# A spectral filter with a gated convolution on one core: inverse-transform pairs and double-block gate taps

## The chip, the cores and the metric

One Trainium2 chip, one of its cores. The metric is device microseconds of one execution of the whole program; a kernel's time is the median of its runs.

## What is computed

The input `x` is 8 sequences of 3200 positions with 256 features. Each sequence goes through a real Fourier transform over positions, a complex 256x256 matrix product with a bias in the frequency domain, a soft threshold, and the inverse transform; the result is then gated and projected:

```python
X = np.fft.rfft(x, axis=1)
Yr = Xr @ w_r - Xi @ w_i + b_r
Yi = Xr @ w_i + Xi @ w_r + b_i
Yr = np.sign(Yr) * np.maximum(np.abs(Yr) - 0.01, 0.0)
Yi = np.sign(Yi) * np.maximum(np.abs(Yi) - 0.01, 0.0)
y = np.fft.irfft(Yr + 1j * Yi, n=3200, axis=1)
gate_pre = sum(conv_w[k] * y_shifted_by(4 - k) for k in range(5))   # causal, per feature
out = ((1 / (1 + np.exp(-gate_pre))) * (y @ w_val)) @ w_out
```

All of it is in float32; the wide products run on rounded high and low parts.

## The kernel before, in words

The length 3200 is split as 64 x 50, so each transform has two steps with a transposition through DRAM between them. For each sequence:

- `p1` (8 pieces): the 50-point step. Matmuls on half of the array (L541) into a PSUM tile `p`, an ACT copy (L546) to `s`, a store to `a_dram`.
- `p2` (13 pieces `u`: 12 of two frequencies, a last one of one): load `a`, the 64-point step `s` (L588), the split of its result into high and low parts (`sx`, `xs`, L638 to L650, on ACT and DVE), the frequency product `k_ps` and `y_ps` (L663, L658), bias and sum on DVE (L669, L672), the soft threshold `tp` (an ACT relu, L676, and a DVE operation, L678), the 64-point step back `z_ps` (L694, 64x64 tiles of the array; L687 for the last piece), an ACT copy to `z_t` (L699) and a store to `z_dram`.
- `positions` (8 blocks `k` of 400 positions): load `zl`, the 50-point step back `y_p` (L746), an ACT copy into `y_sb` (L753). The last block is computed first, since the causal window of block 0 begins with its end (the turn: L759, L765).
- `gated` (8 blocks): split of the block into `y_hl`, value product `v_ps` (L778, or L774 with whole float32 weights for the last blocks of the program), five taps per feature half into `acc` (the first on ACT, L804; four on DVE, L807), sigmoid (L817, ACT), gate (L819, DVE), split into `gated` (L313, L315), projection `o_ps` (L778), copy (L843), store.

Nothing runs in the order in which it is written. `Plan` collects all pieces, each with a due place `at`, an assumed duration and its dependences; `Plan.order` then lists them engine by engine: the piece that can begin first, and of those that begin about together the one that is due first. The table `O` holds the offsets of the due places (in units of one `u`), `SLOTS` the number of buffers per kind. Five kinds of PSUM tile, `p`, `z_ps`, `y_p`, `v_ps` and `o_ps`, rotate through the two buffers of `ps_2`. Pieces of mode "q" use tiles of 64 rows of the array (`p`, `z_ps`, `y_p`), all others the whole array. Stages of neighbouring sequences overlap: while sequence b is in `p2`, b+1 is in `p1` and b-1 in `gated`. `WARM` says how many matmuls on zeros keep TensorE busy in five places of the start (L871).

Of the kernel before, what the change touches and what calls it, by code (L numbers as in the profile page):

```python
# [213 lines left out]
CLOCK = ((40000, 1.6), (55000, 1.15))  # L214
# [37 lines left out]
WARM = 2, 1, 1, 1, 6
SLOTS = {"x": 3, "zl": 3, "y_hl": 2, "s1": 2, "a": 3, "xs": 2, "sx": 2, "xz": 1, "yb": 2, "tp": 2, "zst": 3,
# [7 lines left out]
def fourier_filter_then_gated_conv(ctx: ExitStack, tc: tile.TileContext, x, w_r, w_i, b_r, b_i,  # L261
# [300 lines left out]
    def p2(b, u, at):  # L562
# [119 lines left out]
        gs = [("g1", ts[0], 0)]  # L682

        def s1i():
            p = two_banks(kz)
# [3 lines left out]
            g = g1_sb[:, ts[0] * P:(ts[0] + 2) * P].rearrange("p (r q) -> p r q", r=2)

            for r in range(2):
                for i in range(2):
                    for e in range(2):
                        nc.tensor.matmul(p[e * HP:(e + 1) * HP, i, 0:D], g[i * HP:(i + 1) * HP, r, e * HP:(e + 1) * HP],  # L694
                                         tl[kt][i * HP:(i + 1) * HP, r, :], start=r == 0, stop=r == 1)
        add(at + O["s1i"], "PE", 430 if last else 914, s1i, [kt + (0,), *gs], [kz + (0,)], {kz: "ps_2"}, mode="f" if last else "q")
# [83 lines left out]

    def gated(b, k, at):
        bk = (b, k)
        here, there = [("y", k, 0)], [("y", k - 1, j) for j in range(3 if k == 0 else 1)]
        ky, kg, kv, kh, kp, ko = (("y_hl", bk), ("acc", bk), ("v_ps", bk), ("gated", bk), ("o_ps", bk), ("o", bk))
# [3 lines left out]
        else:  # L788
# [10 lines left out]
        acc = lambda c: tl[kg][:, c, :]  # L799

        def first(c):
            if c == 0:
                buffer(kg, "acc", [P, 2, TB])
            nc.scalar.mul(block(acc(c)), y_at(k, c, 0), cw_sb[:, c, 0:1])  # L804

        def tap(c, j):
            nc.vector.scalar_tensor_tensor(out=block(acc(c)), in0=y_at(k, c, j), scalar=cw_sb[:, c, j:j + 1],  # L807
                                           in1=block(acc(c)), op0=ALU.mult, op1=ALU.add)
        for c in range(2):
# [137 lines left out]
```

## Time and profile before

| | |
|---|---|
| median of 3 runs (lowest to highest) | 911.27 us (909.95 to 912.53) |
| the profiled execution, its own time | 911.79 us |
| span of its trace | 909.7 us |
| mean granted TensorE clock | 0.981 of full speed |
| instructions in the trace | 25018 |
| DMA | 162.30 MB, mean 178 GB/s |

The span runs from the first to the last instruction; the execution's own time has 2.1 us more around it. Engines: PE is TensorE, PEld its weight load, DVE VectorE, ACT ScalarE, POOL GpSimd, SP the engine that issues most transfers. Busy time is the union of an engine's instructions; bars of neighbouring instructions overlap by their start-up, so what one costs is read from the distance between starts.

### The profile page before, as it was taken

The numbers are of one execution on the slowest core, as the hardware profiler recorded it, in microseconds if no ns is written. First come the engines' busy times: TensorE is split into PE (matmuls) and PEld (weight loads), VectorE is DVE, ScalarE is ACT, GpSimd is POOL, SyncE is SP. The second block draws the span as 40 slices with busy tenths as digits, with TensorE's granted clock in tenths as the row PEclk, the third lists the DMA queues.
The fourth block names the chain that finished last, engine by engine and source line by source line (L and its number), as shares of the span: only waits on it lengthen the run. The fifth ranks groups of instructions, "written<-read, shape, count | busy, mean of one in ns | idle before, by whom it ended". The sixth has DMA issues, their size and how long they took to land.

```text
span 909.7 us, 25018 instructions
## 1 busy us (share of the span) xinstructions
PE 875.9 (96%) x10362; PEld 739.8 (81%) x10362; DVE 793.9 (87%) x1387; ACT 628.9 (69%) x1096; POOL 4.3 (0%) x11
## 2 busy tenths in 40 slices
PE   7899989999999999999999999999999999999997
PEld 2478767888888979898888888888888998998765
DVE  1256887999998997999799997999889998999796
ACT  1356556878777777877678766877677766876664
POOL 0000000000000000000000000000001000000000
PEclk8799999999999999999999999999999999999999
DMA  6677767544774466735766376644764344423412
GB/s 202 210 247 232 198 208 247 195 157 162 248 242 149 136 217 201 232 129 164 232 209 198 111 226 214 211 159 147 240 203 145 125 154 145 136 74 130 151 60 90
DMA packets 104212, 162.30 MB, mean 178 GB/s; under 512 B 9922, under 2 KB 78404, under 8 KB 104100
## 3 DMA queue, kind: packets, MB, share of 16 engines
q1 hardware_dynamic: 103140, 157.44, 54.3%
q10 hardware_dynamic: 960, 3.28, 1.1%
q8 instruction: 81, 1.33, 0.7%
q14 instruction: 31, 0.25, 0.1%
HBM read 82.04 MB, written 78.64 MB: 177 GB/s over the span
## 4 chain that ended last, share of the span: by engine, by line
PE 45%; DVE 41%; ACT 5%; issue 4%; DMA 3%; ACTq 0%; SPq 0%; DVEq 0%
DVE acc L807 16%; PE y_ps L658 8%; PE o_ps L778 7%; PE v_ps L778 6%; PE s L588 6%; PE z_ps L694 5%; PE k_ps L663 4%; DVE acc L819 4%; PE p L541 3%; PE y_p L746 3%; DVE gated L315 3%; DVE yb L669 3%; DVE yb L672 3%; DVE y_hl L315 2%; DVE xs L646 2%
## 5 line engine op out<-in xcount | busy, mean ns | idle before, releaser
L807 DVE SCALAR_TENSOR_TENSOR acc<-y_sb,cw_sb,acc 128x400 f32<-128x400 f32 x512 | 301.5, 640 | 3.6 <-ACT acc L804 3.4
L778 PE MATMUL o_ps<-gated,wo_sb 128*128 128x400 f32 x756 | 155.2, 355 | 4.0 <-ACT z_t L699 2.5
L658 PE MATMUL y_ps<-w_sb,xs 128*128 128x256 f32 x1152 | 151.7, 281 | 0.2 <-DVE yb L672 0.2
L778 PEld LDWEIGHTS o_ps<-gated,wo_sb 128*128 128x128 f32 x756 | 136.7, 191 | 12.2 <-ACT z_t L699 6.3
L658 PEld LDWEIGHTS y_ps<-w_sb,xs 128*128 128x128 f32 x1152 | 145.3, 190 | 1.6 <-DVE tp L678 0.8
L778 PE MATMUL v_ps<-y_hl,wv_sb 128*128 128x400 f32 x660 | 133.1, 350 | 2.5 <-ACT s L546 0.9
L588 PEld LDWEIGHTS s<-f_sb,a 128*128 128x128 f32 x800 | 102.6, 193 | 35.9 <-issue 24.4
L778 PEld LDWEIGHTS v_ps<-y_hl,wv_sb 128*128 128x128 f32 x660 | 117.1, 188 | 5.8 <-ACT z_t L699 1.6
L588 PE MATMUL s<-f_sb,a 128*128 128x128 f32 x800 | 118.8, 287 | 1.8 <-DMA a<-a_dram 1.8
L694 PE MATMUL z_ps<-tp,g_sb 64*64 64x256 f32 x1536 | 106.2, 393 | 4.3 <-DVE tp L678 4.3
L676 ACT ACTIVATE tp<-yb,nlam 128x512 f32<-128x512 f32 (+1 forms) x104 | 73.5, 706 | 39.9 <-DVE yb L672 38.8
L313 ACT CAST gated<-acc 128x800 fp32r<-128x800 f32 x63 | 54.3, 862 | 55.5 <-DVE acc L819 55.1
L663 PE MATMUL k_ps<-w_sb,xs 128*128 128x256 f32 x576 | 91.2, 294 | 0.0
L678 DVE SCALAR_TENSOR_TENSOR tp<-yb,tp 128x512 f32<-128x512 f32 (+1 forms) x104 | 69.9, 673 | 20.9 <-ACT tp L676 20.8
L817 ACT ACTIVATE acc<-acc 128x400 f32<-128x400 f32 x128 | 67.9, 539 | 25.5 <-DVE acc L807 24.5
L699 ACT COPY z_t<-z_ps 128x512 f32<-128x512 f32 (+1 forms) x104 | 58.7, 565 | 35.7 <-PE z_ps L694 31.6
L663 PEld LDWEIGHTS k_ps<-w_sb,xs 128*128 128x128 f32 x576 | 75.8, 191 | 8.6 <-issue 4.0
L804 ACT ACTIVATE acc<-y_sb,cw_sb 128x400 f32<-128x400 f32 x128 | 75.6, 626 | 10.5 <-DVE gated L315 10.5
L746 PEld LDWEIGHTS y_p<-g_sb,zl 50*64 50x64 f32 x4096 | 68.3, 136 | 17.1 <-ACT z_t L699 6.3
L672 DVE TENSOR_TENSOR yb<-y_ps,yb 128x512 f32<-128x512 f32 x96 | 66.4, 692 | 10.9 <-PE y_ps L658 10.4
L694 PEld LDWEIGHTS z_ps<-tp,g_sb 64*64 64x64 f32 x1536 | 50.3, 134 | 30.4 <-DVE tp L678 3.9
L746 PE MATMUL y_p<-g_sb,zl 50*64 50x50 f32 x4096 | 70.8, 219 | 4.2 <-DVE acc L819 2.2
(79 smaller groups left out, 1027.9 us busy)
## 6 DMA issues: line engine op xcount, KB each, us to landing
zl<-z_dram SPq DMA_DIRECT2D x128, 200.0 KB
out<-o SPq DMA_DIRECT2D x63, 400.0 KB
a<-a_dram SPq DMA_DIRECT2D x96, 256.0 KB
z_dram<-z_t SPq DMA_DIRECT2D x96, 256.0 KB
x<-in_x SPq DMA_DIRECT2D x120, 200.0 KB
a_dram<-s SPq DMA_DIRECT2D x120, 200.0 KB
x<-in_x ACTq DMA_DIRECT2D x8, 200.0 KB
a_dram<-s ACTq DMA_DIRECT2D x8, 200.0 KB
```

Source lines behind the costliest of these rows:

```text
L588: nc.tensor.matmul(spec()[:, c, :, i, :], tl[ka][:, i, c * P:(c + 1) * P], f2_of(i), start=True, stop=True)
L658: nc.tensor.matmul(p[:, 1 - r, :], xm(hx, c, r), w_sb[:, m, hw, c, :], start=k == 0, stop=k == 5)
L663: nc.tensor.matmul(p, sm(hx, c), w_sb[:, 0, hw, c, :], start=k == 0, stop=k == 5)
L672: add(at + 0.2, "DVE", dve(2 * D), lambda: nc.vector.tensor_tensor(out=yb(), in0=tl[ky], in1=yb(), op=ALU.add), [ky + (0,)], [kb + (0,)])
L676: nc.scalar.activation(out=buffer(kt, "tp", [P, 2, D])[:, 0:n], in_=tl[kb][:, 0:n], func=AF.Relu, bias=nlam)
L678: add(at + 0.2, "DVE", dve(n * D), lambda: nc.vector.scalar_tensor_tensor(out=tl[kt][:, 0:n], in0=tl[kb][:, 0:n], scalar=LAM, in1=tl[kt][: ...
L694: nc.tensor.matmul(p[e * HP:(e + 1) * HP, i, 0:D], g[i * HP:(i + 1) * HP, r, e * HP:(e + 1) * HP], tl[kt][i * HP:(i + 1) * HP, r, :], star ...
L746: nc.tensor.matmul(pv[h][e * HP:(e + 1) * HP, c, m, :], zt[half(h), m, c * P + e * HP:c * P + (e + 1) * HP], g2_sb[half(h), :], start=True ...
L778: nc.tensor.matmul(p[:, e, 0:TB], w[:, hw, c, e * P:(e + 1) * P], src(hy, c), start=n == 0, stop=n == 5)
L804: nc.scalar.mul(block(acc(c)), y_at(k, c, 0), cw_sb[:, c, 0:1])
L807: nc.vector.scalar_tensor_tensor(out=block(acc(c)), in0=y_at(k, c, j), scalar=cw_sb[:, c, j:j + 1], in1=block(acc(c)), op0=ALU.mult, op1=A ...
L817: add(at + O["conv"] + 0.15, "ACT", act(TB, "sigmoid"), lambda c=c: nc.scalar.activation(out=acc(c), in_=acc(c), func=AF.Sigmoid), (), [kg ...
```

## The change

Three things change, and the order with them.

1. The step back is made for two pieces at once. For even `u` nothing is issued; for odd `u` one PSUM tile takes 16 matmuls (of `u - 1` and `u`), one ACT copy moves 1024 elements instead of two that move 512, and one store carries 512 KB instead of two of 256 KB. The 13th piece stays alone.
2. The gate's taps and sigmoid run over two neighbouring blocks: `acc` holds 2 x 2 x 400 elements per partition, each tap and each sigmoid has 800 elements instead of 400. The gate's product, the split and the projection stay per block. The last two blocks of the last sequence stay single.
3. The offsets in `O`, the number of warm-up matmuls in the last of the five places (6 to 10), two buffer counts (`tp` 2 to 3, `zst` 3 to 2, the latter now twice as large) and the planner's assumptions on the clock are other numbers, and `gated` is entered two blocks at a time.

```diff
-CLOCK = ((40000, 1.6), (55000, 1.15))
+CLOCK = ((40000, 1.6), (45000, 1.15))
...
-O = {'hold': 0.0, 'together': 2.0, 'later': 4.0,
+O = {'hold': -1.089,
+     'together': 2.272,
+     'later': 4.406,
...
-     's1i': 1.087,
+     's1i': 1.333,
...
-     'conv': 1.033,
-     'val': 1.634,
-     'gate': -3.715,
-     'project': 3.74,
+     'conv': 1.176,
+     'val': 2.74,
+     'gate': -3.751,
+     'project': 5.91,
...
-WARM = 2, 1, 1, 1, 6
...
+WARM = 2, 1, 1, 1, 10
...
+        if u % 2 == 0 and not last:
+            return
+
+        both = (u,) if last else (u - 1, u)
+        kts = [("tp", (b, v)) for v in both]
...
+            for j, v in enumerate(both):
+                g = g1_sb[:, 2 * v * P:(2 * v + 2) * P].rearrange("p (r q) -> p r q", r=2)
+
+                for r in range(2):
+                    for i in range(2):
+                        for e in range(2):
+                            nc.tensor.matmul(p[e * HP:(e + 1) * HP, i, j * D:(j + 1) * D],
+                                             g[i * HP:(i + 1) * HP, r, e * HP:(e + 1) * HP],
+                                             tl[kts[j]][i * HP:(i + 1) * HP, r, :], start=r == 0, stop=r == 1)
...
-            nc.scalar.copy(out=buffer(ko, "zst", [P, 2, D])[:, 0:n], in_=tl[kz][:, 0:n, 0:D])
+            zt = buffer(ko, "zst", [P, 4, D])
...
+            nc.scalar.copy(out=zt.rearrange("p (j i) d -> p i j d", i=2), in_=tl[kz].rearrange("p i (j d) -> p i j d", j=2))
...
-            dst = tl[kd].rearrange("q (m c) -> (q m) c", c=D).rearrange("(t r) c -> r t c", r=P)
-            nc.sync.dma_start(out=dst[:, ts[0]:ts[-1] + 1, :], in_=tl[ko][:, 0:n])
...
+            nc.sync.dma_start(out=dst[:, t0:t0 + nz, :], in_=tl[ko][:, 0:nz])
...
+    def blocks_at_once(b, k):
+        return 1 if b == B - 1 and k >= NB - 2 else 2
+
+    def taps(b, k, nb, at):
...
+        def y_of(c, tap):
+            lo = (k * MB + tap) * N2
+            return y_sb[:, c, :, lo:lo + nb * MB * N2]
...
+            nc.scalar.mul(acc(c), y_of(c, 0), cw_sb[:, c, 0:1])
+
+        def tap(c, j):
+            nc.vector.scalar_tensor_tensor(out=acc(c), in0=y_of(c, j), scalar=cw_sb[:, c, j:j + 1],
+                                           in1=acc(c), op0=ALU.mult, op1=ALU.add)
...
+        gate = lambda: tl[kg][:, :, :, (k - k0) * MB * N2:(k - k0 + 1) * MB * N2]
...
-            if i:
-                gated(b, k, start + (i - 1) * T / NB)
+            nb = blocks_at_once(b, k)
+            if i and (nb == 1 or k % 2):
+                for j in range(k + 1 - nb, k + 1):
+                    gated(b, j, start + (i - 1 - k + j) * T / NB)
```

How this moves instructions is seen in three places. PE, in the middle of a sequence, first as it was (`p` is the first step of the next sequence, `s` to `y_ps` the current one, `v_ps` and `o_ps` the gating of the one before):

```order
L658 MATMUL y_ps<-w_sb,xs 128x256 x12
L694 MATMUL z_ps<-tp,g_sb 64x256 x8
L541 MATMUL p_4071<-x,f_sb 64x512 x4
L588 MATMUL s_4084<-f_sb,a 128x2x64 x4
L663 MATMUL k_ps<-w_sb,xs 128x256 x6
L778 MATMUL v_ps<-y_hl,wv_sb 128x400 x12
L658 MATMUL y_ps<-w_sb,xs 128x256 x12
L694 MATMUL z_ps<-tp,g_sb 64x256 x8
L541 MATMUL p_4160<-x,f_sb 64x512 x4
L588 MATMUL s_4171<-f_sb,a 128x2x64 x4
```

The same place of a sequence in the changed program:

```order
L543 MATMUL p_5269<-x,f_sb 64x512 x4
L660 MATMUL y_ps<-w_sb,xs 128x256 x12
L703 MATMUL z_ps<-tp,g_sb 64x256 x16
L543 MATMUL p_5322<-x,f_sb 64x512 x4
L665 MATMUL k_ps<-w_sb,xs 128x256 x6
L590 MATMUL s_5343<-f_sb,a 128x2x64 x4
L791 MATMUL o_ps<-gated,wo_sb 128x400 x12
L660 MATMUL y_ps<-w_sb,xs 128x256 x12
L791 MATMUL v_ps<-y_hl,wv_sb 128x400 x12
L665 MATMUL k_ps<-w_sb,xs 128x256 x6
L590 MATMUL s_5425<-f_sb,a 128x2x64 x4
```

`z_ps` comes half as often and twice as long; `p` no longer always stands beside it. Over the whole program the array's tiling changes 228 times before and 192 times after, in a sequence of the middle 26 and 22 times.

DVE at the end of the program, from the last sequence's last threshold (`tp` of 256 elements) on, before:

```order
L678 SCALAR_TENSOR_TENSOR tp<-yb,tp 128x256
L807 SCALAR_TENSOR_TENSOR acc<-y_sb,cw_sb,acc 128x400 x4
L315 TENSOR_TENSOR y_hl<-y_sb,y_hl 128x800
L807 SCALAR_TENSOR_TENSOR acc<-y_sb,cw_sb,acc 128x400 x4
L819 TENSOR_TENSOR acc<-v_ps,acc 128x800
L807 SCALAR_TENSOR_TENSOR acc<-y_sb,cw_sb,acc 128x400 x3
L315 TENSOR_TENSOR gated<-acc,gated 128x800
```

And in the changed program:

```order
L680 SCALAR_TENSOR_TENSOR tp<-yb,tp 128x256
L317 TENSOR_TENSOR y_hl<-y_sb,y_hl 128x800
L317 TENSOR_TENSOR gated<-acc,gated 128x800
L813 SCALAR_TENSOR_TENSOR acc<-y_sb,cw_sb,acc 128x800 x3
L855 TENSOR_TENSOR acc<-v_ps,acc 128x4x200
L813 SCALAR_TENSOR_TENSOR acc<-y_sb,cw_sb,acc 128x800 x2
L317 TENSOR_TENSOR gated<-acc,gated 128x800
```

From that threshold to the program's end DVE had 84 taps of 400 elements, 11 gates and 11 splits (one `y_hl`, ten `gated`); now it has 31 taps of 800 and 16 of 400, 11 gates and 12 splits (one `y_hl`, eleven `gated`).

PE at the start, from the last warm-up on (`s_245` and `s_240` are the first spectrum matmuls, which wait for the first load of `a`), before:

```order
L871 MATMUL warm<-idle 128x512 x6
L447 MATMUL bias_223<-b_sb 128x256 x4
L449 MATMUL bias_224<-b_sb 128x256 x2
L588 MATMUL s_245<-f_sb,a 128x2x64 x4
L541 MATMUL p_263<-x,f_sb 64x512 x4
L663 MATMUL k_ps<-w_sb,xs 128x256 x6
L658 MATMUL y_ps<-w_sb,xs 128x256 x12
```

And in the changed program:

```order
L907 MATMUL warm<-idle 128x512 x10
L590 MATMUL s_240<-f_sb,a 128x2x64 x2
L449 MATMUL bias_243<-b_sb 128x256 x4
L451 MATMUL bias_244<-b_sb 128x256 x2
L590 MATMUL s_240<-f_sb,a 128x2x64 x2
L590 MATMUL s_257<-f_sb,a 128x2x64 x4
L543 MATMUL p_270<-x,f_sb 64x512 x4
L543 MATMUL p_284<-x,f_sb 64x512 x4
L665 MATMUL k_ps<-w_sb,xs 128x256 x6
```

The bias matmuls have moved behind the first half of the first spectrum burst, and a second spectrum burst and a second `p` stand ahead of the first product.

## Rows read from the trace of the kernel before

**Rows 1.** Page, busy time of PE and DVE: us, share of the span, instructions.

```profile
PE 875.9 (96%) x10362; PEld 739.8 (81%) x10362; DVE 793.9 (87%) x1387; ACT 628.9 (69%) x1096; POOL 4.3 (0%) x11
```

**Rows 2.** Page, the chain that ended last: shares by engine, then by line.

```profile
PE 45%; DVE 41%; ACT 5%; issue 4%; DMA 3%; ACTq 0%; SPq 0%; DVEq 0%
DVE acc L807 16%; PE y_ps L658 8%; PE o_ps L778 7%; PE v_ps L778 6%; PE s L588 6%; PE z_ps L694 5%; PE k_ps L663 4%; DVE acc L819 4%; PE p L541 3%; PE y_p L746 3%; DVE gated L315 3%; DVE yb L669 3%; DVE yb L672 3%; DVE y_hl L315 2%; DVE xs L646 2%
```

**Rows 3.** Busy time by stretch: stretch, length, engines (instructions), clock, DMA share, GB/s.

```profile
346.62:451.05 104.43, 103.43 (x1294) 90.77 (x1297) 96.51 (x168) 78.14 (x137) 0.00 (x0) 1.00 0.59 189
...
850.00:903.00 53.00, 48.32 (x500) 36.43 (x501) 49.02 (x79) 33.11 (x52) 0.00 (x0) 0.97 0.27 91
```

**Rows 4.** The chain in order of time, 340 to 460 us: start, us, what.

```profile
346.62 2.01 PE y_p L746 x128
...
353.81 1.40 PE y_ps L658 x12
...
451.05 2.01 PE y_p L746 x128
```

**Rows 5.** PE in order of time, 412 to 424 us: start, us, [idle before, releaser].

```profile
415.75 2.46 PE L778 MATMUL o_ps<-gated,wo_sb 128*128 128x400 f32 x12 [0.71 <-ACT z_t L699]
```

**Rows 6.** DVE in order of time, 400 to 425 and 840 to 909.7 us.

```profile
420.52 0.68 DVE L646 TENSOR_TENSOR xs<-s,xs 128x512 fp32r<-128x512 f32 x1
421.12 0.42 DVE L650 TENSOR_TENSOR xs<-sx,xs 128x256 fp32r<-128x256 f32 x1
...
842.14 0.98 DVE L315 TENSOR_TENSOR gated<-acc,gated 128x800 fp32r<-128x800 f32 x1
843.04 1.72 DVE L807 SCALAR_TENSOR_TENSOR acc<-y_sb,cw_sb,acc 128x400 f32<-128x400 f32 x3
...
849.95 5.56 DVE L807 SCALAR_TENSOR_TENSOR acc<-y_sb,cw_sb,acc 128x400 f32<-128x400 f32 x10 [0.75 <-ACT acc L804]
```

**Rows 7.** ACT in order of time, 296 to 312 us.

```profile
303.96 0.57 ACT L699 COPY z_t<-z_ps 128x512 f32<-128x512 f32 x1
304.43 0.97 ACT L817 ACTIVATE acc<-acc 128x400 f32<-128x400 f32 x2
305.29 0.81 ACT L753 COPY y_sb<-y_p 128x800 f32<-128x800 f32 x1
...
310.97 0.63 ACT L804 ACTIVATE acc<-y_sb,cw_sb 128x400 f32<-128x400 f32 x1
311.50 1.00 ACT L546 COPY s<-p 128x1024 f32<-128x1024 f32 x1
```

**Rows 8.** PE in order of time, 800 to 850 us, at changes of the array's tiling.

```profile
804.51 1.56 PE L658 MATMUL y_ps<-w_sb,xs 128*128 128x256 f32 x12
806.00 1.09 PE L694 MATMUL z_ps<-tp,g_sb 64*64 64x256 f32 x16
807.03 1.16 PE L588 MATMUL s<-f_sb,a 128*128 128x128 f32 x8
...
810.32 1.09 PE L694 MATMUL z_ps<-tp,g_sb 64*64 64x256 f32 x16
811.23 1.10 PE L746 MATMUL y_p<-g_sb,zl 50*64 50x50 f32 x64
```

**Rows 9.** The start: PE in order of time, 0 to 75 us, and one stretch.

```profile
27.72 5.93 PE L871 MATMUL warm<-idle 128*128 128x512 f32 x12
33.76 1.96 PE L447 MATMUL bias<-b_sb 1*128 1x256 f32 x8
35.56 1.68 PE L449 MATMUL bias<-b_sb 1*128 1x256 f32 x4
39.08 2.08 PE L588 MATMUL s<-f_sb,a 128*128 128x128 f32 x8 [1.85 <-DMA a<-a_dram]
...
40.00:45.00 5.00, 4.54 (x14) 1.45 (x13) 1.36 (x3) 1.27 (x3) 0.00 (x0) 0.50 0.90 240
```

More of the change, by code (lines that the diff above doesn't have):

```diff
@@ L681, in p2 @@
         kz, ko, kd = ("z_ps", bu), ("z_t", bu), ("z_dram", b)
-        gs = [("g1", ts[0], 0)]
+        if u % 2 == 0 and not last:
+            return
+        both = (u,) if last else (u - 1, u)
+        kts = [("tp", (b, v)) for v in both]
+        gs = [("g1", 2 * v, 0) for v in both]
+        nz = 1 if last else 4
         def s1i():
@@ L688, in s1i @@
                 return
[L689 to L696, printed above, removed]
@@ L701, in store @@
+        add(at + O["s1i"], "PE", 430 if last else 1776, s1i, [*[k + (0,) for k in kts], *gs], [kz + (0,)], {kz: "ps_2"}, mode="f" if last else "q")
+        def keep():
+            zt = buffer(ko, "zst", [P, 4, D])
+            if last:
+                nc.scalar.copy(out=zt[:, 0], in_=tl[kz][:, 0, 0:D])
+                return
+            nc.scalar.copy(out=zt.rearrange("p (j i) d -> p i j d", i=2), in_=tl[kz].rearrange("p i (j d) -> p i j d", j=2))
         def store():
-            if u == 0:
+            if u == 1:
@@ L710, in fourier_filter_then_gated_conv @@
+            nc.sync.dma_start(out=dst[:, t0:t0 + nz, :], in_=tl[ko][:, 0:nz])
+        add(at + O["s1i"] + 0.1, "ACT", act(nz * D), keep, [kz + (0,)], [ko + (0,)], {ko: "zst"})
+        add(at + O["s1i"] + 0.11, "SP", 400, store, [ko + (0,)], [kd + (v,) for v in both], {kd: "z_dram"} if u == 1 else None,
+            kb=128 * nz)
     w_late = {}
     H0 = KC - 1
-    def block(ap):
-        return ap.rearrange("p (h n) -> p h n", h=NH)
     def y_at(k, c, tap=H0):
@@ L793, in gated @@
             vm = lambda e: matrix(kv, e, wv_sb, lambda h, c: tl[ky][:, h, c, :], False)
+        if k == k0:
+            vs = [*vs, *[("y", j, 0) for j in range(k + 1, k + nb)]]
         for e in range(2):
@@ L796, in gated @@
                 {kv: "ps_2"} if e == 0 else None, chain="val")
[L799 to L809, printed above, removed]
-            add(at + O["conv"] + 0.01 * c, "ACT", act(TB, "conv"), lambda c=c: first(c), [*here, *there, ("cw", 0, 0)],
-                [kg + (c,)], {kg: "acc"} if c == 0 else None, chain="conv")
@@ L812, in gated @@
-        for j in range(1, KC):
-            for c in range(2):
-                add(at + O["conv"] + 0.02 * j, "DVE", dve(TB), lambda c=c, j=j: tap(c, j), [*here, *there], [kg + (c,), *([("turn", "read", (b, c))] if (k, j) == (NB - 1, KC - 1) else [])],
-                    delay=545 + (130 if j == KC - 1 else 0))
-        for c in range(2):
-            add(at + O["conv"] + 0.15, "ACT", act(TB, "sigmoid"), lambda c=c: nc.scalar.activation(
-                out=acc(c), in_=acc(c), func=AF.Sigmoid), (), [kg + (c,)])
+        kg = ("acc", (b, k0))
```

65 lines of the change are left out of this document (43 added, 22 removed).

## The prediction

> **What bounds the kernel now.** I read the busy shares first, then the chain of waits, then one period of the middle, then the two ends. TensorE is busy for 96% of the span and VectorE for 87% [rows 1], so neither rules alone, and the chain of waits says so outright: 45% of it is PE, 41% DVE, 5% ACT, and one line, the gate's taps (L807), holds 16% [rows 2]. The middle repeats: the double burst of `y_p` that begins at 346.62 us begins again at 451.05 us [rows 4], so a sequence costs 104.43 us there. In that period PE has a matmul in flight for 103.43 us and DVE works 96.51 us [rows 3]. Matmul bars overlap, so a wait can hide in a full PE row: at 415.75 us the projection still sat 0.71 us behind an ACT copy that freed its PSUM buffer [rows 5]. After 850 us it is plainly DVE's program: 49.02 us of work in 53.00 us [rows 3]. The price of an instruction below is the distance to the next start, not the bar, since bars overlap.
>
> **Taps over two blocks.** A 512-element DVE operation is followed 0.60 us later (420.52 to 421.12) and an 800-element one 0.90 us later (842.14 to 843.04) [rows 6]: 1.04 ns per element and 0.07 us fixed. Ten taps in a row last 5.56 us and one bar is 0.63 us, so a 400-element tap costs (5.56 - 0.63) / 9 = 0.548 us; 0.417 us of it is elements, 0.131 us is fixed [rows 6]. No tap of 800 elements is in this trace. If the whole 0.131 us is paid once per instruction, it costs 0.131 + 0.833 = 0.964 us, and a merge saves 0.131 us; if only the 0.07 us of the other operations is fixed, it saves 0.07 us. I take 0.131 us: the larger operations lie on one line with an equal slope, so nothing points to a slower element. There are 512 taps; the last two blocks of the last sequence stay single, so 248 pairs merge and 248 instructions go: 248 x 0.131 = 32.5 us of DVE (17.4 us at the other bound). The Trainium skill (Perfetto Trace Analysis, section Optimizing Scalar/DVE Operations) gives about 60 ns of access overhead for a DVE instruction on SBUF, and by that figure, as an estimate, the merge would save 248 x 0.06 = 15 us; the tap rows show twice that overhead, so the rows are used.
>
> What of this lies on the path? The taps' 16% of the chain is 146 us. The end is counted by itself. In the order after the last sequence's last threshold (the second order piece), DVE has 84 taps, 11 gates and 11 splits of 800 before; in the changed program 31 double taps, 16 single ones, 11 gates and 12 splits. That is 84 x 0.548 = 46.0 us against 31 x 0.964 + 16 x 0.548 = 38.7 us, and one more split of 0.90 us: 6.4 us less in a stretch where DVE sets the pace. I take 5 us, because a pair can begin only when two blocks are evacuated. The bounds are 2 and 6.4 us. The other 100 us of taps on the chain shrink by 0.131 / 1.096 = 12%, 12 us; when a DVE stretch shortens, PE, which has something in flight nearly all the time [rows 3], becomes the later one in part of it. I take 7 us, bounds 0 and 26 (all that is left of 32.5 us).
>
> **ACT.** The first tap costs 0.53 us for 400 elements (310.97 to 311.50), the sigmoid 0.43 us (two in 304.43 to 305.29) [rows 7]; at 0.83 ns per element the fixed parts are 0.20 and 0.10 us. 62 of each go: 18.6 us. The `z_t` copy costs 0.47 us for 512 elements [rows 7]; for 1024, by the 1024-element bar's 1.00 us against 0.57 us, it costs 0.90 us, so 48 merges save 2 us. Only 5% of the chain is ACT [rows 2]: I take 1 us, bounds 0 and 3.
>
> **The transform back in pairs, and the order.** `y_ps` followed by 64x64 work costs 1.49 us (804.51 to 806.00) against 1.40 us in the chain [rows 4, 8]; `z_ps` followed by 128x128 work costs 1.03 us (806.00 to 807.03), by more 64-row work 0.91 us (810.32 to 811.23) [rows 8]. So a change of the array's tiling costs about 0.1 us each way. The orders have 228 such changes before and 192 after (in a middle sequence 26 and 22): 36 x 0.105 = 3.8 us of PE. The matmuls are the same, so nothing else goes there. PE is on the path about half of the time, and a little more once DVE is lighter: 2.5 us, bounds 0 and 3.8. The 96 paired stores become 48 of twice the size; what follows them, the loads of `zl`, waited for all of a sequence's stores already, and the last one stays single, so I cost this at nothing. Its cover is the gating of the sequence before; without it the next load would start later by the extra copy time, 0.43 us per sequence.
>
> **The start.** Four more warm-up matmuls are eight more records; twelve took 6.04 us (27.72 to 33.76) [rows 9], so these end near 37.8 us, still before 39.08 us, when the first spectrum matmuls get their `a`: hidden. But the bias matmuls, 33.76 to 37.2 us before, now stand behind the first half of that burst (third order piece) and delay its second half by up to 3.4 us. Against it: the granted clock in 40 to 45 us is 0.50 [rows 9], the 1.2 GHz level, after bias matmuls on one row and a wait; with longer warm-up it may stand at 2.4 GHz there and return up to 5 us. I take 0, bounds -5 and +3.4.
>
> **The sum** against the profiled execution: 7 + 5 + 1 + 2.5 = 15.5 us. That execution took 911.79 us (span 909.7, so 2.1 us lie around it), 0.5 us above the median of 911.27 us. 911.79 - 15.5 - 0.5 gives 895.8, said as **896 us**.
>
> **Rivals.**
> - *PE takes over at once* (0.14). PE's 103.43 of 104.43 us [rows 3] speaks for it: shorter DVE stretches only uncover full PE ones. Left are the end's 5 us and 3 us of PE: 904 us, between 901 and 908. Against it: the hidden wait of [rows 5] and 41% of the chain on DVE.
> - *DVE is the whole bound* (0.11). All of the 32.5 us and the PE's 3.8 us arrive: 875 us, 874 to 886. Against it: PE's 45% of the chain does not shrink by 12%.
> - *The merge saves nothing that counts* (0.08): the tap's extra 0.06 us is per element, and the coarser steps eat the rest. 908.5 to 914 us.
> - *The pair holds PSUM, slower* (0.13). `p`, `z_ps`, `y_p`, `v_ps` and `o_ps` share two rotating PSUM buffers. A first block's `v_ps` sits in one until its gate, and that now waits for a tap that is 0.42 us longer and for two sigmoids that are 0.33 us longer each: 1.1 us per pair, 31 pairs, 34 us. Each `z_ps` holds the other 0.43 us longer, 48 times, 21 us. If PE sees half of these 55 us, the time is 911 - 15.5 + 27 = 923 us; it decides once more than 28% is seen. For it: the 0.71 us of [rows 5] is exactly such a wait. Against it: `z_ps` takes 48 turns fewer in that ring, DVE reaches each gate with less work ahead, and the offsets put the value and projection matmuls later. The Trainium skill (Perfetto Trace Analysis, Optimizing Scalar/DVE Operations) sides with this rival: where Scalar or Vector are not saturated but cause bubbles on other engines, it advises breaking instructions up. By that rule this change goes the wrong way; no trace here shows it either way yet.
>
> **How the numbers follow.** The forecast case (0.54) runs from 886 to 904 us by the bounds of the middle's term. With a measurement able to tell about 0.3% (2.7 us), faster means under 908.5 us: 0.54 + 0.14 + 0.11 = 0.79. Within 0.3%: 0.08. Slower: 0.13. Eight in ten lie between 879 us, which takes in part of the DVE-bound case, and 912 us, which leaves out the slower case and part of the even one.
>
> **What would show it.** Right: 264 taps, mean bars near 1.05 us for 800 elements and starts 0.96 us apart; DVE busy near 762 us; the period of the middle at 102 to 103.5 us; the end from the last threshold shorter by about 5 us; 192 tiling changes. Wrong: a period of 104.4 us or more with new waits of `o_ps`, `v_ps` or `z_ps` on ACT copies or on the gate (held PSUM); a period under 100.5 us (DVE was the bound); taps spaced 1.03 us (the extra is per element); the first `k_ps` more than 2 us later than now (the bias matmuls cost the start).

## The result, and the profile after

| | before | after |
|---|---|---|
| median (lowest to highest) | 910.88 us (909.95 to 912.53, 4 runs) | 897.96 us (894.13 to 901.98, 4 runs) |
| ratio to before, 95% interval | 1 | 0.9857 [0.981, 0.9904] |
| profiled execution: time, span, mean clock | 911.79 us, 909.7 us, 0.981 | 898.98 us, 897.1 us, 0.986 |

The changed kernel is 1.4% faster, 12.9 us (the interval lies below 1), and lies 2 us from the 896 us of the forecast. The page after, busy time, chain by engine and by line, and the group of the taps (line, engine, operation, tiles, forms, count; busy us, mean ns of both forms; idle before and its releaser):

```profile
PE 865.2 (96%) x10370; PEld 741.1 (83%) x10370; DVE 763.5 (85%) x1139; ACT 603.7 (67%) x924; POOL 4.4 (0%) x11
...
PE 83%; DVE 10%; DMA 4%; ACT 2%; issue 1%; ACTq 1%; SPq 0%
...
L813 DVE SCALAR_TENSOR_TENSOR acc<-y_sb,cw_sb,acc 128x800 f32<-128x800 f32 (+1 forms) x264 | 255.9, 1018 | 17.6 <-ACT acc L810 17.2
```

Against [rows 1, 2]: DVE lost 30.4 us of busy time and ACT 25.2 us, and the chain has gone over to PE, from 45% to 83%. VectorE is no longer what ends last, except near the end. A run of eight taps at the end of the program:

```profile
841.96 7.78 DVE L813 SCALAR_TENSOR_TENSOR acc<-y_sb,cw_sb,acc 128x800 f32<-128x800 f32 x8
```

One bar of 800 elements is 1.04 us (the mean of the 248), so starts are (7.78 - 1.04) / 7 = 0.963 us apart; the prediction had worked out 0.964 us. Middle period and end, each as a stretch (the columns are those of [rows 3]):

```profile
514.30:617.40 103.10, 102.01 (x1292) 90.85 (x1291) 92.87 (x137) 75.53 (x115) 0.00 (x0) 1.00 0.60 193
...
821.40:897.10 75.70, 66.70 (x750) 51.67 (x750) 61.91 (x76) 41.68 (x55) 0.00 (x0) 0.99 0.35 117
```

The same two stretches before, from the start of a sequence's last threshold (DVE `tp` of 256 elements) to that of the next, and from the last one to the end of the span:

```profile
521.50:625.90 104.40, 103.41 (x1292) 90.74 (x1291) 96.48 (x170) 78.11 (x137) 0.00 (x0) 1.00 0.60 190
...
828.70:909.70 81.00, 69.25 (x752) 52.84 (x751) 68.25 (x112) 47.01 (x74) 0.00 (x0) 0.98 0.33 112
```

This period is 1.3 us shorter and the end 5.3 us. These thresholds are the milestones of all runs below. Where they start, in us, in the profiled execution of each (`pairs`: the transform back for two pieces; `double`: taps over two blocks; `numbers`: offsets, warm-up, planner's clock):

| sequence | 1 | 2 | 3 | 4 | 5 | 6 | 7 | 8 | from the 8th to the end |
|---|---|---|---|---|---|---|---|---|---|
| before | 117.1 | 206.5 | 310.8 | 417.0 | 521.5 | 625.9 | 732.8 | 828.7 | 81.0 |
| after | 114.3 | 210.2 | 308.9 | 410.7 | 514.3 | 617.4 | 724.1 | 821.4 | 75.7 |
| pairs, old numbers | 118.4 | 207.5 | 309.0 | 412.4 | 515.8 | 619.1 | 724.3 | 822.0 | 81.7 |
| pairs, new numbers, single taps | 113.5 | 207.7 | 304.9 | 407.2 | 510.5 | 613.6 | 717.2 | 815.3 | 83.4 |
| double, old numbers | 119.6 | 207.9 | 325.8 | 437.5 | 547.9 | 659.5 | 770.3 | 869.6 | 88.2 |

Read by parts, the changed program is 3.7 us behind at the 2nd threshold, gains 12.4 us from the 2nd to the 7th (513.9 us instead of 526.3), loses 1.4 us from the 7th to the 8th and gains 5.3 us from there to the end. Each row is one execution of one order.

What TensorE waited for between 320 and 760 us (line, releaser: us in total, times, longest), before:

```profile
PE o_ps L778 <- ACT z_t L699: 2.1, 3, 0.7
PE p L541 <- DVE acc L819: 1.9, 2, 1.2
PE v_ps L778 <- ACT s L546: 0.9, 3, 0.3
PE y_p L746 <- ACT z_t L699: 0.3, 1, 0.3
```

and after:

```profile
PE y_p L759 <- issue: 3.9, 3, 1.5
PE k_ps L665 <- DVE yb L671: 0.9, 1, 0.9
```

In this stretch all waits for a buffer of `ps_2` (freed by an ACT copy or by the gate) are gone, `o_ps` on the `z_t` copy of [rows 5] among them. Behind the last threshold they are still there (`y_p` on the gate: 2.2 us in both programs). What has come is a gap inside a burst of `y_p` which nothing in the trace releases; before there was one such gap in the whole program, 1.5 us, near its end.

### The profile page after: what moved, and what is told of

The parts are those of the page before. It is cut to its first block, busy times and chain, and to the rows that moved or that the text cites. A ratio compares the mean times of both kernels' runs of the same rounds, so it can differ in the third digit from the quotient of the medians.

```text
span 897.1 us, 24381 instructions
## 1 busy us (share of the span) xinstructions
PE 865.2 (96%) x10370; PEld 741.1 (83%) x10370; DVE 763.5 (85%) x1139; ACT 603.7 (67%) x924; POOL 4.4 (0%) x11
## 4 chain that ended last, share of the span: by engine, by line
PE 83%; DVE 10%; DMA 4%; ACT 2%; issue 1%; ACTq 1%; SPq 0%
PE y_ps L660 14%; PE o_ps L791 13%; PE v_ps L791 12%; PE s L590 10%; PE z_ps L703 9%; PE k_ps L665 8%; PE y_p L759 7%; PE p L543 6%; DVE acc L813 4%; DMA x<-in_x 1%; PE v_ps L787 1%; DVE acc L855 1%; DVE gated L317 1%; DMA f_sb<-in_f 1%; DMA a_dram<-s 1%
## 5 line engine op out<-in xcount | busy, mean ns | idle before, releaser
L813 DVE SCALAR_TENSOR_TENSOR acc<-y_sb,cw_sb,acc 128x800 f32<-128x800 f32 (+1 forms) x264 | 255.9, 1018 | 17.6 <-ACT acc L810 17.2
L660 PE MATMUL y_ps<-w_sb,xs 128*128 128x256 f32 x1152 | 155.4, 284 | 0.6 <-DVE xs L648 0.6
L791 PEld LDWEIGHTS o_ps<-gated,wo_sb 128*128 128x128 f32 x756 | 133.5, 188 | 3.1 <-DVE acc L855 0.8
L791 PE MATMUL v_ps<-y_hl,wv_sb 128*128 128x400 f32 x660 | 131.3, 346 | 0.5 <-ACT o L879 0.5
L590 PE MATMUL s<-f_sb,a 128*128 128x128 f32 x800 | 113.2, 284 | 8.2 <-ACT wo_sb L315 3.4
L703 PE MATMUL z_ps<-tp,g_sb 64*64 64x256 f32 x1536 | 93.4, 381 | 0.0
L671 DVE TENSOR_TENSOR yb<-k_ps,bias_sb 128x512 f32<-128x512 f32 x96 | 65.6, 684 | 15.7 <-PE k_ps L665 15.6
L703 PEld LDWEIGHTS z_ps<-tp,g_sb 64*64 64x64 f32 x1536 | 55.3, 133 | 27.4 <-issue 5.1
L855 DVE TENSOR_TENSOR acc<-v_ps,acc 128x800 f32<-128x800 f32 x64 | 62.9, 984 | 16.1 <-PE v_ps L791 12.7
L714 ACT COPY z_t<-z_ps 128x1024 f32<-128x1024 f32 x48 | 48.5, 1010 | 25.7 <-PE z_ps L703 25.1
```

Of the source, the lines that this page charges most:

```text
L590: nc.tensor.matmul(spec()[:, c, :, i, :], tl[ka][:, i, c * P:(c + 1) * P], f2_of(i), start=True, stop=True)
L660: nc.tensor.matmul(p[:, 1 - r, :], xm(hx, c, r), w_sb[:, m, hw, c, :], start=k == 0, stop=k == 5)
L671: nc.vector.tensor_tensor(out=buffer(kb, "yb", [P, 2, D]), in0=tl[kk].rearrange("p (a d) -> p a d", a=1).to_broadcast([P, 2, D]), in1=bias ...
L703: nc.tensor.matmul(p[e * HP:(e + 1) * HP, i, j * D:(j + 1) * D], g[i * HP:(i + 1) * HP, r, e * HP:(e + 1) * HP], tl[kts[j]][i * HP:(i + 1) ...
L791: nc.tensor.matmul(p[:, e, 0:TB], w[:, hw, c, e * P:(e + 1) * P], src(hy, c), start=n == 0, stop=n == 5)
L813: nc.vector.scalar_tensor_tensor(out=acc(c), in0=y_of(c, j), scalar=cw_sb[:, c, j:j + 1], in1=acc(c), op0=ALU.mult, op1=ALU.add)
```

## The experiments

### The three parts, each alone and in twos

Six programs fill up the table of which part does what. In each the planner makes the order anew.

**Pairs alone** (before, with the paired transform back and its two buffer counts):

```diff
 # before
-SLOTS = {"x": 3, "zl": 3, "y_hl": 2, "s1": 2, "a": 3, "xs": 2, "sx": 2, "xz": 1, "yb": 2, "tp": 2, "zst": 3,
+SLOTS = {"x": 3, "zl": 3, "y_hl": 2, "s1": 2, "a": 3, "xs": 2, "sx": 2, "xz": 1, "yb": 2, "tp": 3, "zst": 2,
...
+        if u % 2 == 0 and not last:
+            return
+
+        both = (u,) if last else (u - 1, u)
...
```

> The kernel before with the transform back in pairs (and its buffer counts) and nothing else of the change: old offsets, old warm-ups, single taps; the planner orders it anew and gets 190 tiling changes. Theory (the pairs shorten PE by 3.8 us of tiling changes and some 2.5 us inside the double bursts, and PE sets the pace): 902 to 908 us. Rival (the pairs need the new offsets, as the single transform back needed the old ones): 912 to 930 us.

Measured: 904.51 us (903.26 to 905.46), ratio 0.9914 [0.9892, 0.9937]. The pairs by themselves bring 7.8 us, as the theory had it, with VectorE as loaded as before (791.8 us busy); TensorE's busy time fell from 875.9 to 867.7 us. From the 2nd to the 7th threshold 526.3 us became 516.8 us. TensorE's waits between 320 and 760 us are 3.7 us against 5.2 us before; `o_ps` on the `z_t` copy is 0.3 us of it instead of 2.1:

```profile
PE o_ps L792 <- ACT z_t L712: 0.3, 2, 0.2
```

**Double taps alone** (before, with taps over two blocks):

```diff
 # before
+    def blocks_at_once(b, k):
+        return 1 if b == B - 1 and k >= NB - 2 else 2
...
+            nb = blocks_at_once(b, k)
+            if i and (nb == 1 or k % 2):
+                for j in range(k + 1 - nb, k + 1):
+                    gated(b, j, start + (i - 1 - k + j) * T / NB)
```

> The kernel before with double taps (and gating entered by pairs of blocks) and nothing else of the change: old offsets, old warm-ups, single transform back; the planner orders it anew and gets 242 tiling changes. Theory (double taps shorten the end, the middle is PE's): 903 to 911 us. Rival (double taps relieve DVE all along): 885 to 898 us. Rival (the old offsets do not fit pairs of blocks): 915 to 930 us.

Measured: 958.73 us (954.74 to 961.68), ratio 1.0507 [1.047, 1.0543]: 46 us slower, though DVE has 27 us less to do, and slower than any of the three expectations. VectorE first, in this kernel's trace in order of time:

```profile
592.89 7.78 DVE L797 SCALAR_TENSOR_TENSOR acc<-y_sb,cw_sb,acc 128x800 f32<-128x800 f32 x8
600.59 0.41 DVE L645 TENSOR_TENSOR sx<-s,sx 128x256 f32<-128x256 f32 x1
600.92 0.68 DVE L646 TENSOR_TENSOR xs<-s,xs 128x512 fp32r<-128x512 f32 x1
```

TensorE at the same time:

```profile
597.87 1.05 PE L588 MATMUL s<-f_sb,a 128*128 128x128 f32 x8
601.70 2.05 PE L588 MATMUL s<-f_sb,a 128*128 128x128 f32 x8 [2.79 <-ACT acc L808]
```

The busy times of two neighbouring stretches; the granted clock is the third column from the end:

```profile
594.00:601.00 7.00, 4.92 (x35) 4.73 (x33) 7.00 (x9) 3.85 (x7) 0.00 (x0) 1.00 0.45 137
601.00:608.00 7.00, 6.30 (x35) 3.78 (x36) 5.76 (x10) 4.19 (x8) 0.00 (x0) 0.52 0.21 62
```

Eight double taps stand in a row on DVE, 7.8 us, and the split of an `s` that TensorE had long finished (`sx`, `xs`) stands behind them. `s` has two PSUM buffers (`ps_s2`), and the burst at 601.70 needs the one which that split still reads until 601.60. (The view names an ACT sigmoid, which ended at 601.57 but does not touch `s`; the buffer is the reading that fits the program.) So TensorE waits 2.79 us, and behind the wait its clock is granted at 0.52 of full speed, the 1.2 GHz level: the same eight `s` matmuls take 2.05 us instead of 1.05. Per period there are two such runs of eight (592.89 and 626.74). `s` waited four times in 440 us for 11.1 us, `y_ps` four times for 6.7 us; from the 3rd threshold to the 7th a period costs 110 to 112 us.

The changed program has a run of six or eight in each period too, but TensorE's order covers it. VectorE's run, from the trace after:

```profile
561.37 7.79 DVE L813 SCALAR_TENSOR_TENSOR acc<-y_sb,cw_sb,acc 128x800 f32<-128x800 f32 x8 [2.28 <-ACT acc L810]
569.08 0.42 DVE L647 TENSOR_TENSOR sx<-s,sx 128x256 f32<-128x256 f32 x1
```

and TensorE beside it:

```profile
561.31 1.65 PE L660 MATMUL y_ps<-w_sb,xs 128*128 128x256 f32 x12
562.80 2.36 PE L791 MATMUL o_ps<-gated,wo_sb 128*128 128x400 f32 x12
565.09 1.96 PE L703 MATMUL z_ps<-tp,g_sb 64*64 64x256 f32 x32
566.86 1.10 PE L759 MATMUL y_p<-g_sb,zl 50*64 50x50 f32 x64
567.89 0.71 PE L590 MATMUL s<-f_sb,a 128*128 128x128 f32 x4
568.36 2.43 PE L791 MATMUL v_ps<-y_hl,wv_sb 128*128 128x400 f32 x12
```

No row of it carries a wait: for 7.8 us PE has work that needs nothing from VectorE, or what VectorE had finished earlier.

**Both, with the old offsets** (the changed program with the table `O` of before; the warm-up and the planner's clock stay new):

```diff
 # after
-     'conv': 1.176,
-     'val': 2.74,
-     'gate': -3.751,
-     'project': 5.91,
...
+     'conv': 1.033,
+     'val': 1.634,
+     'gate': -3.715,
+     'project': 3.74,
...
```

> The changed code with the table of offsets of the kernel before (pairs, double taps, new buffer counts and warm-up kept). It is the run with the pairs alone plus double taps, and the run with the taps alone plus pairs. If double taps placed by the old offsets block VectorE (runs of eight, 7.7 us, ahead of the splits that TensorE waits for), it is slow with the pairs too: 930 to 955 us, with waits of PE s and PE y_ps on DVE and ACT in the middle. If the 46 us of the run with the taps alone came from the single transform back not fitting, it is 896 to 906 us.

Measured: 969.94 us (965.53 to 977.98), ratio 1.0648 [1.0603, 1.0694], slower than either part alone and than the 930 to 955 us expected. From 320 to 760 us there are twelve unbroken stretches of taps of over 4 us, where the taps alone had eight and the changed program four. The waits are the same ones (TensorE's, 320 to 740 us):

```profile
PE s L588 <- ACT acc L822: 11.3, 4, 3.0
PE y_ps L658 <- DVE yb L672: 9.6, 4, 2.4
```

**New numbers alone** (before with the new table, warm-up, clock assumption and `tp` 3):

```diff
 # before
-O = {'hold': 0.0, 'together': 2.0, 'later': 4.0,
...
+O = {'hold': -1.089,
+     'together': 2.272,
+     'later': 4.406,
...
-WARM = 2, 1, 1, 1, 6
...
+WARM = 2, 1, 1, 1, 10
...
```

> The kernel before with the changed kernel's offsets, warm-ups, clock assumption and buffer counts, but single transform back and single taps: 264 tiling changes. Theory (the merged instructions bring the gain, the numbers only fit them): no gain, 909 to 918 us. Rival (the new offsets bring the gain by themselves): 896 to 904 us.

Measured: 922.32 us (917.32 to 924.19), ratio 1.0102 [1.0055, 1.015]. The numbers are no gain by themselves; the loss is some 4 us more than the theory's 918 us.

**New numbers and double taps, single transform back**:

```diff
 # after
-        if u % 2 == 0 and not last:
-            return
-
-        both = (u,) if last else (u - 1, u)
...
```

> The changed kernel with the transform back made piece by piece as before (matmuls, copy and store), double taps and all other numbers as changed; the planner orders it anew and gets 262 tiling changes instead of 192. Theory: 70 x 0.105 = 7.4 us of PE and 2 us of ACT more: 901 to 907 us. Rival (only DVE counts): 896 to 899 us. Rival (the pairs hold the PSUM ring and cost): under 896 us.

Measured: 929.79 us (927.63 to 932.04), ratio 1.0191 [1.016, 1.0222]. None of the expectations reached so far; the time lies 23 us above the theory's 907 us, so the tiling changes on TensorE and the copies on ACT do not price this part.

**New numbers and pairs, single taps**:

```diff
 # after
     def blocks_at_once(b, k):
-        return 1 if b == B - 1 and k >= NB - 2 else 2
+        return 1
```

> The changed kernel with every block gated alone (taps, first tap and sigmoid of 400 elements), pairs of the transform back and all numbers as changed; the planner orders it anew. Theory: DVE and ACT are back at their old loads (32.5 and 18.6 us more), PE keeps its 192 to 196 tiling changes: 904 to 911 us, some 3 us under the kernel before. Rival (the merged taps bring nothing, PE's order all): 896 to 900 us. Rival (DVE is the whole bound): about the kernel before, 908 to 912 us.

Measured: 903.04 us (900.52 to 905.43), ratio 0.9897 [0.9865, 0.9929], within 1 us of the theory's 904 to 911 us. The chain by engine:

```profile
PE 73%; DVE 17%; DMA 4%; ACT 4%; issue 1%; ACTq 0%; SPq 0%
```

The same period and the end, as stretches:

```profile
510.50:613.60 103.10, 102.60 (x1294) 90.90 (x1292) 96.87 (x170) 77.42 (x131) 0.00 (x0) 1.00 0.60 193
...
815.30:898.70 83.40, 69.75 (x764) 53.49 (x762) 71.56 (x117) 48.38 (x76) 0.00 (x0) 0.99 0.33 112
```

VectorE works 96.87 us in the period, as much as before, and the period is 103.10 us, as in the changed program. By the 7th threshold this program is 7 us ahead of the changed one (717.2 against 724.1); the end, 7.7 us longer, gives that back.

Together, as ratios to before:

| | single transform back | pairs |
|---|---|---|
| old numbers, single taps | 1 | 0.9914 |
| old numbers, double taps | 1.0507 | 1.0648 |
| new numbers, single taps | 1.0102 | 0.9897 |
| new numbers, double taps | 1.0191 | 0.9857 |

Double taps lose in three of the four places (5.1, 7.4 and 0.9%); only with pairs and new numbers do they gain, 0.4%, and there the two intervals overlap: a gain from them is not shown. Pairs gain 0.9, 2.0 and 3.3%, and lose, 1.3%, only where the double taps stand on the old offsets. Each cell is one order of the planner (and 1.0648 has the new warm-up and planner's clock): two orders below, which differ in the taps of one sequence alone, lie 11 us apart, so a few microseconds between two cells need not belong to the part that differs.

### Weights added and taken away in the changed program's own order

Here the order is kept and single instructions are made heavier or lighter.

**Each double tap as two single ones, one behind the other** (DVE 32.5 us heavier):

```diff
 # after
-            nc.vector.scalar_tensor_tensor(out=acc(c), in0=y_of(c, j), ...
+            for v in range(nb):
+                at_v = slice(v * MB * N2, (v + 1) * MB * N2)
+                nc.vector.scalar_tensor_tensor(out=acc(c)[:, :, at_v], in0=y_of(c, j)[:, :, at_v], ...
```

> The changed kernel in its own order, with every double tap issued as two taps of 400 elements one behind the other: PE and ACT have the same instructions in the same order, DVE has 248 instructions more. At 0.131 us each that is 32.5 us more of DVE. Theory (DVE's relief counts fully at the end, in the middle only until PE takes over): the end from the last threshold 5 to 6 us longer, the middle 0.5 to 1.2 us per sequence longer, in all 904 to 911 us. Rival (DVE is the whole bound): 25 to 32 us longer, 923 to 930 us. Rival (PE is the whole bound): no more than the end's 5 us, 898 to 903 us.

Measured: 927.7 us (919.97 to 929.5), ratio 1.0152 [1.0101, 1.0202]: by the medians 30 of the 32.5 us arrive, by the two ratios 27. Taken alone, this says that VectorE is the whole bound, as the rival's 923 to 930 us have it; it holds 55% of this chain.

**The third tap left out** (62 instructions of 0.96 us and four single ones; DVE's busy time falls by 57 us):

```diff
 # after
         def tap(c, j):
+            if j == 2:
+                return
```

> The changed kernel in its own order; the third of the five taps of every block is left out, so one tap's term is missing from the gate. 66 DVE instructions go, about 62 us of DVE. Theory now (in the middle of the changed kernel PE sets the pace, DVE only the end): the sequences of the middle keep their 103 us within 0.5 us, the end shortens by 5 to 8 us: 886 to 893 us. Rival (DVE sets the middle's pace too, as the in-place split suggests): 7 to 8 us per sequence less, 840 to 855 us.

Measured: 900.4 us (898.7 to 903.31), ratio 0.9873 [0.9845, 0.9902]. Nothing is gained over the changed program in the total; the expected 886 to 893 us did not come. Its page, busy times and chain:

```profile
PE 867.4 (97%) x10370; PEld 744.3 (83%) x10370; DVE 706.3 (79%) x1073; ACT 602.5 (67%) x924; POOL 4.4 (0%) x11
...
PE 87%; DVE 5%; DMA 4%; ACT 2%; issue 1%; ACTq 0%; SPq 0%
```

and its middle period:

```profile
512.70:615.30 102.60, 102.06 (x1292) 90.91 (x1291) 85.92 (x129) 75.27 (x115) 0.00 (x0) 1.00 0.60 193
```

VectorE's 92.87 us of the period became 85.92 us and the period went from 103.10 to 102.60 us: PE has 102 us to do in either. Up to the 7th threshold this program is 4.6 us ahead (719.5 against 724.1 us). It loses that again behind it, 178.3 us instead of 173.0, though VectorE has less to do. One stretch of it, and the same one of the changed program:

```profile
840.00:860.00 20.00, 17.57 (x237) 14.55 (x228) 12.03 (x14) 9.99 (x13) 0.00 (x0) 0.83 0.31 104
...
840.00:860.00 20.00, 18.36 (x304) 14.38 (x296) 19.93 (x22) 13.71 (x18) 0.00 (x0) 1.00 0.41 132
```

So the 0 of the total is a small gain in the middle and a loss at the end, where the clock was granted at 0.83 instead of 1.00 for this stretch; how much of the loss is the clock's was not tried.

**The value product two terms long instead of three** (PE 40 us lighter by the expectation's count of matmuls; its busy time falls by 25 us):

```diff
 # after
+        few = key[0] == "v_ps"
...
-            for hw, hy in ((0, 0), (1, 0), (0, 1)):
...
+            for hw, hy in ((0, 0), (0, 1)) if few else ((0, 0), (1, 0), (0, 1)):
...
```

> The changed kernel in its own order; the value product leaves out its term with the weights' low part (4 of 12 matmuls of every block that is not computed with whole weights). That is 4 x 0.18 = 0.72 us of PE per block, 5.8 us per sequence, 55 blocks, 40 us. Theory (PE sets the pace): the sequences of the middle fall from 103 us to 97 to 98.5 us, in all 862 to 872 us. Rival (DVE sets the pace, PE waits inside its bursts): they stay above 101 us, 885 to 897 us.

Measured: 893.13 us (886.74 to 895.74), ratio 0.9785 [0.9729, 0.984]: 5 to 7 of 40 us, as the rival had it. The chain goes straight back to VectorE:

```profile
DVE 51%; PE 31%; ACT 8%; issue 5%; DMA 4%; ACTq 1%; SPq 0%; DVEq 0%
```

and `y_ps` now waits for VectorE's sum (TensorE's waits, 320 to 760 us):

```profile
PE y_ps L660 <- DVE yb L674: 5.3, 9, 1.2
PE y_p L759 <- issue: 4.5, 4, 2.0
```

The three runs belong together. In this order PE is the last to finish, and VectorE stands right behind it: VectorE made 32.5 us heavier costs 27 to 30, VectorE with 57 us less busy time brings 0 in all (under 5 up to the 7th threshold), and PE made 40 us lighter brings 5 to 7.

### The end

**Double taps only in the last sequence**, and **only in the last two** (new numbers and pairs in both, order made anew):

```diff
 # after
     def blocks_at_once(b, k):
-        return 1 if b == B - 1 and k >= NB - 2 else 2
+        return 2 if b == B - 1 and k < NB - 2 else 1
```

```diff
 # after
-        return 1 if b == B - 1 and k >= NB - 2 else 2
+        return 2 if b >= B - 2 and (b, k) < (B - 1, NB - 2) else 1
```

> The changed program with its numbers, but taps over two blocks only for the first six blocks of the last sequence; everywhere else single taps (DVE about 28 us heavier than in the changed program). Theory A (in the middle TensorE sets the pace whatever the taps cost; double taps pay only in the end, where VectorE sets it): middle periods between last thresholds 103 to 104 us as with single taps throughout, the end from the last threshold 76 to 79 us instead of 83.4, time 893 to 899 us. Theory B (double taps pay in the middle, as the prediction had it, 7 us): time 903 to 906 us, the end shorter but the middle longer than in the changed program by 1 us per period.

> As the run before, with double taps in the last two sequences. Theory A: within 3 us of it, 893 to 900 us, since the sequence before the last lies in the middle, where TensorE sets the pace. Theory B: about 1 us less than the run before for the sequence that is added. A third case: the order is made anew, and a planner's order may miss by several us either way; then this run and the one before differ by more than 4 us though their work differs by 4 us of VectorE alone.

Measured: the last sequence alone 909.23 us (907.14 to 913.62), ratio 0.9973 [0.9958, 0.9988]; the last two 897.99 us (895.38 to 902.98), ratio 0.9849 [0.9819, 0.9879]. Up to the 7th threshold the two agree (714.9 and 714.2 us), with periods of 102.4 to 103.5 us on single taps. Then the first takes 193.2 us to the end and the second 185.3 us: the third case of the expectation, an order that misses. The first one's end, TensorE in order of time:

```profile
851.74 1.15 PE L759 MATMUL y_p<-g_sb,zl 50*64 50x50 f32 x64 [0.94 <-ACT y_sb L766]
854.29 1.96 PE L759 MATMUL y_p<-g_sb,zl 50*64 50x50 f32 x64 [1.40 <-DVE acc L855]
856.18 4.95 PE L787 MATMUL v_ps<-y_sb,w_late 128*128 128x400 f32 x8
```

and one stretch of it:

```profile
833.00:877.00 44.00, 34.50 (x582) 26.54 (x581) 30.39 (x35) 22.18 (x28) 0.00 (x0) 0.77 0.24 76
```

The planner put blocks of `y_p` one behind the other, so that TensorE waits for a PSUM buffer ahead of each, 0.94 us for the copy of a block and 1.40 us for a gate; the clock is granted at 0.77 on average over 44 us, and the eight matmuls of `v_ps` that take 2.85 us elsewhere (at 863.14 in this trace) take 4.95 us. The changed program in the same stretch of time:

```profile
833.00:877.00 44.00, 40.62 (x642) 32.04 (x643) 40.01 (x47) 28.50 (x37) 0.00 (x0) 1.00 0.34 113
```

So the theory that double taps pay just in the end fits one of the two runs and fails for the other: what the end costs is a matter of its order and of the clock too, and not of the taps' price alone. No version that computes everything beats the changed kernel: the last two sequences alone give the same time, with 56 merged instructions instead of 248.

### The start

**Six warm-up matmuls in the last place instead of ten**, in the changed program's order:

```diff
 # after
-        for _ in range(n):
+        for _ in range(min(n, 6)):
```

> The changed program in its own order, with six warm-up matmuls instead of ten in the last place (eight records fewer). If the warm-up holds the clock up: the stretch at half the clock from 42.65 us becomes 10 to 14 us long instead of 6.8, the first sequence's last threshold starts at 116 to 118 us instead of 114.3, and the program is 0 to 3 us slower (898 to 901 us), since what the start gains is given back by the second threshold. If it does nothing: the half-clock stretch stays 6.8 us and the time within 2 us of the changed program's.

Measured: 899.56 us (895.24 to 902.31), ratio 0.9863 [0.9838, 0.9888]; not told apart from the changed program in the total. The start is. TensorE after:

```profile
28.35 9.07 PE L907 MATMUL warm<-idle 128*128 128x512 f32 x20
39.42 0.71 PE L590 MATMUL s<-f_sb,a 128*128 128x128 f32 x4 [1.99 <-DMA a<-a_dram]
40.06 1.99 PE L449 MATMUL bias<-b_sb 1*128 1x256 f32 x8
```

and the stretch from 40 to 45 us:

```profile
40.00:45.00 5.00, 4.20 (x18) 3.07 (x16) 0.00 (x0) 1.72 (x4) 0.00 (x0) 0.76 0.83 217
```

With six:

```profile
26.77 5.32 PE L907 MATMUL warm<-idle 128*128 128x512 f32 x12
41.38 1.22 PE L590 MATMUL s<-f_sb,a 128*128 128x128 f32 x4 [9.30 <-DMA a<-a_dram]
42.54 3.78 PE L449 MATMUL bias<-b_sb 1*128 1x256 f32 x8
```

and the same stretch:

```profile
40.00:45.00 5.00, 3.62 (x10) 2.92 (x11) 0.00 (x0) 0.00 (x0) 0.00 (x0) 0.50 0.97 242
```

With a wait of 9.30 us instead of 1.99 us the clock stands at its lower level, 1.2 GHz, from 35 to 50 us (granted 0.50, where the changed program has 1.00, 0.76 and 0.55 in the three stretches of 5 us), which is longer than the 10 to 14 us expected; the bias matmuls take 3.78 us instead of 1.99. (`a` itself landed later in this execution, so part of the difference is not the clock's.) The first threshold starts at 116.7 us instead of 114.3, the third at 312.5 instead of 308.9; by the end 1.5 us of that is left between the two spans (898.6 and 897.1).

## Why the prediction was right, and where its steps were not

The time is within the range and close to the figure. The price of a tap and the figure for the end came out as worked out. Two other terms were wrong by some microseconds in opposite directions: that the sum is as close as it is was luck. The lower edge of the range, 886 us, does not follow from the bound of 26 us that is named for it: that would give 877 us.

**The price of a tap**: right. 0.963 us against 0.964, 264 instructions, DVE busy 763.5 us where 762 was expected. The whole 0.131 us is paid once per instruction, and the rival by which the extra is per element is out.

**Seven microseconds from taps on the chain in the middle**: this step failed. The prediction took the taps' 16% of the chain [rows 2] and shrank it. With pairs and new numbers, single and double taps have the same period of 103.10 us between the 5th and the 6th threshold, and leaving out a whole tap changes that period by 0.5 us. Between the 2nd and the 7th threshold single taps even took 509.5 us and double ones 513.9 us. A chain names the engine that was last, not by how much; the runs suggest that in the old chain, too, the two engines were about equally late where VectorE stood on it, but no run made VectorE lighter in the order of before. In these executions the value was thus at the prediction's bound of 0 or 4 us below it.

**Pairs, 2.5 us on the path**: the mechanism was right, the size was not. Measured alone, 7.8 us. The words "the matmuls are the same, so nothing else goes there" are the error. One burst of 32 followed by 64-row work takes 565.09 to 566.86, 1.77 us, where two of 16 took 2 x 0.91 us [rows 8]: 0.05 us a pair, 2.4 us in all. The order with pairs alone has 190 changes of tiling instead of 228, 38 x 0.105 = 4.0 us. Waits fell by 1.5 us between 320 and 760 us. The sum of these is 7.9 us, and TensorE's busy time fell by 8.2 us; that they add up is an argument, and that all of it lies on the path was not tried part by part. The chain of that run does not say so: PE holds 43% of it and DVE 39%. So that the pairs bring more than 2.5 us is measured; why nearly all of TensorE's relief arrives stays open.

**The end, 5 us**: 5.3 us measured (81.0 to 75.7), in the profiled executions. The prediction's reason, fewer instructions on VectorE, is shown in part only. Against single taps with the same numbers the end is 7.7 us shorter; but with still lighter taps it is 78.6 us, and with double taps in the last sequence alone 93.7 us. The order and the granted clock can move it by more than the taps do.

**The start, 0**: the prediction's two effects both exist, but they did not leave 0. (Its 5 us for the clock in 40 to 45 us was too wide: 5 us at half the clock can return 2.5 us.) The clock was granted at 0.76 in 40 to 45 us instead of 0.50 [rows 9]; the first `k_ps` came at 50.50 us instead of 45.12. That lateness was named as a sign that the start had lost. More spectrum and first-step work stands ahead of it, and the first threshold came 2.8 us earlier all the same. By the second threshold, however, the changed program was 3.7 us behind, by the third 1.9 us ahead; what took the 6.5 us between the first two was not tried. Single taps with the same numbers are 1.2 us behind there.

**ACT, 1 us**: its busy time fell by 25.2 us where 20.6 us was worked out; no run isolates its share of the path.

**The rivals.** *PE takes over at once* is the mechanism that came true (83% of the chain), at less time than the 901 us at the edge of its range. TensorE itself became shorter by more than this rival's 3 us: its busy time fell by 10.7 us. *DVE is the whole bound* would have been confirmed by the split taps (27 to 30 us more) and is refuted by the tap left out (0) and by single taps in a new order (5 us). *The pair holds PSUM* did not happen in the middle of the changed program: between 320 and 760 us all waits on `ps_2` went. A slower outcome was real, though, by another route: with the old offsets double taps cost 5 to 7%, as an unbroken VectorE run ahead of the splits that TensorE needs. The rule of the Trainium skill (Perfetto Trace Analysis, section Optimizing Scalar/DVE Operations), that breaking instructions up may help where Vector is not saturated but causes bubbles on other engines, agrees with that: 904.51 us with single taps, 969.94 us with double ones on the old offsets. With the new numbers it does not show: 903.04 us against 897.96 us.

## What to carry to other kernels

Where two engines are nearly level, as here with 96 and 87% of the span busy, the chain's shares did not price a saving on one of them: make the engine lighter and heavier in the same order, since only the pair of runs shows whether it is the bound or just behind it. Count what a merge takes away on the engine with the least slack (here tiling changes, burst starts and buffer turns on TensorE), even if the merge is meant for another. Longer instructions may need the due places moved with them: the same merge changed the time by between +7.4% and -0.4%, and in the slow order it was what stood behind it in the queue that TensorE waited for. Where a planner makes the order anew, one run per variant prices an order, and not the part that was changed.

## What the runs showed that was not expected

- A short wait of TensorE cost twice. After 2.79 us without work the granted clock was 0.52 over the next 7 us, and eight matmuls took 2.05 us instead of 1.05.
- The changed kernel's runs spread over 7.9 us, those of before over 2.6 us. Its mean granted clock falls as the time rises: 0.989, 0.987, 0.986 and 0.985 in runs of 894.13, 896.94, 898.98 and 901.98 us. The lowest and the highest differ by 0.004, which over 897 us is 3.6 us of full speed, an estimate; that is about half of the spread, and the rest stays open.
- In the changed program's order there are gaps inside a burst of `y_p` that nothing in the trace releases. In 320 to 760 us they come to 3.9 us after, and in the same order to 3.8 us with split taps, 4.5 us with the short value product, 2.5 us with the tap left out and 2.0 us with six warm-ups; in the three other orders with pairs and new numbers, which have single taps in this stretch, they come to 0.8 to 1.2 us, with none over 0.6 us. What the instruction stream waits for there was not tried and stays open. One such gap, in the chain of waits of the changed program in order of time:

```profile
453.55 1.07 PE y_p L759 x60
454.62 1.49 issue
456.10 0.32 PE y_p L759 x3
```
